# Slots and place biases on GpSimd, h in pairs of blocks, copies of x split by side

## The chip, the cores and the metric

One NeuronCore of a Trainium2 chip. In the profile PE is TensorE (matmuls; PEld its weight loads), DVE is VectorE, ACT is ScalarE, POOL is GpSimd and SP is SyncE, which here only issues transfers; ACTq and DVEq are sequencers of those engines. The metric is the time of one execution in device microseconds; the median of several runs counts.

## The reference

Linear attention over 8 batches, 8 heads, 576 positions and 64 columns a head, and then a mixture of 8 experts of which each row takes one.

```
q_s = exp(q - max(q, -1)); q_s /= sum(q_s, -1) + 1e-9      # over the 64 columns
k_s = exp(k - max(k, 2));  k_s /= sum(k_s, 2) + 1e-9       # over the positions
x = (q_s @ (k_s^T @ v)) as rows [4608, 512]
logits = x @ w_gate + modality_bias[modality_id]
e = argmax(logits); g = max(softmax(logits))
out[row] = g[row] * (relu(x[row] @ w1[e[row]]) @ w2[e[row]])   # w1 512x1024, w2 1024x512
```

## The kernel before

The bias of a modality outweighs what x adds to the logits, so the kernel takes one expert for each of the two modalities, loads the weights of these two alone (by registers read from the computed ids), and sorts the rows by modality: side a fills a list of places from the front, side b from the back. A count at the end would repeat work for rows that chose another expert; here its loop runs zero times.

**Attention**, batch by batch (`attention`): q, k and v come by SP in one queue into a ring of five buffers `st`. ScalarE takes the exponentials of q and k, VectorE sums q (L827), VectorE (batches 0 and 1) or GpSimd (later ones) scales q into `eq` (L843), ScalarE or GpSimd casts v into `vb` (L864). TensorE then forms kv (L957), from which VectorE makes `kinv` (L984, L987) and the scaled `kvbd` (L993); it sorts q within a block of 64 positions by a permutation `perm` (S1, L1033), which is cast into `et` (L1045 on ScalarE, L1047 on VectorE), and multiplies by kvbd (S2, L1072). S2 leaves two blocks of 64 positions in one PSUM bank. Each block is copied twice into the sorted `xs` (L1103): to a window of side a and to one of side b, whose starts are register values read from `offp` (L1007).

**Places.** `slot_run` and `digits_run` give each row's place, in two digits; one-hot matrices of the digits (`hhi`, L689, and `hlo`, L677, written into xs where no window lies yet) and their products `hv` with the rows' numbers (GpSimd, L701) go through 36 matmuls (L718) to the list `idx` of rows by place. `bsel_run` gives each place its bias.

**Experts.** 18 passes of 256 places (`ffn`), nine a side: logits (L1138), h in 8 blocks of 128 (L1198; 4 matmuls of 256 columns each, one bank a block) with an eviction by ScalarE (L1172) or VectorE (L1174), whichever the planner finds free, then y in two tiles of 128 rows (L1211; 8 matmuls of 512 columns), scaled by the gate (L1178, L1180) and stored by an indirect transfer of GpSimd (L1183). `ffn_rest` repeats the one block of 128 places that both sides share.

**Order.** All this is written down as operations with costs, a rank and buffers from rings; `Plan.order` runs a list scheduler over them and so fixes each engine's order and each buffer. On the chip every engine takes its list in order and waits by semaphores. A ring of six PSUM banks (a seventh joins) serves all of it. `load_w` asks for weights from GpSimd's queue: the first behind the landing of batch 1's k, the last two of the second expert (`pl.later(o, o_hv[-1])`) behind the last hv.

## Time and profile before

| | us |
|---|---|
| median of 3 runs | 208.88 |
| lowest and highest | 205.66, 209.72 |
| profiled execution | 204.27 |
| its span, first to last instruction | 202.0 |
| PE, DVE, ACT, POOL busy | 178.6, 154.7, 128.0, 90.6 |

The span is that of the profiled execution alone. Busy time says how full an engine is, not what the end waits for; a busy PE can hold matmuls that wait in its pipeline.

### The profile page before, as it was taken

What the parts mean: (1) busy time and instruction counts of PE and PEld (TensorE: products, weight loads), DVE (VectorE), ACT (ScalarE), POOL (GpSimd) and SP (SyncE); (2) the same over time, 40 slices, a digit from 0 to 9 for tenths busy, and PEclk for the clock granted to TensorE, in tenths of its full rate; (3) what the DMA queues carried; (4) which work ended last, traced back from release to release, by engine and by line L of the source; (5) the groups of instructions that cost most, each with busy time, mean ns of one, the idle gap of its engine ahead of it and who ended that gap; (6) DMA issues with size and microseconds to landing.
All of it is one profiled execution on the core that took longest, in us unless ns stands there. A gap on an engine that the chain in (4) does not pass through costs nothing.

```text
span 202.0 us, 5027 instructions
## 1 busy us (share of the span) xinstructions
PE 178.6 (88%) x1735; PEld 122.8 (61%) x1735; DVE 154.7 (77%) x447; ACT 128.0 (63%) x283; POOL 90.6 (45%) x113
## 2 busy tenths in 40 slices
PE   0899559869989899999979979999999999999990
PEld 0446237457656577777566756778667656766760
DVE  2998998997878999685978996869588657755660
ACT  2679886969738689999949966999895000000100
POOL 6000920674843649974098159591303311322231
PEclk9999997999999999999999999999999999999998
DMA  5999999999999997999539922111112112121202
GB/s 196 357 401 395 180 185 209 276 373 321 293 352 405 413 399 272 356 408 396 216 72 394 338 86 79 52 55 55 57 52 104 52 55 104 52 107 54 83 21 109
DMA packets 19612, 42.33 MB, mean 210 GB/s; under 512 B 1913, under 2 KB 3961, under 8 KB 19586
## 3 DMA queue, kind: packets, MB, share of 16 engines
q1 hardware_dynamic: 13344, 28.33, 38.6%
q0 software_dynamic: 6224, 13.64, 24.2%
q8 instruction: 14, 0.23, 0.5%
q10 hardware_dynamic: 18, 0.04, 0.2%
q14 instruction: 12, 0.10, 0.1%
HBM read 36.75 MB, written 9.70 MB: 230 GB/s over the span
## 4 chain that ended last, share of the span: by engine, by line
PE 50%; DMA 23%; DVE 10%; POOL 6%; issue 5%; ACT 3%; ACTq 1%; DVEq 0%; POOLq 0%
PE ps L1211 22%; PE ps L1198 19%; DMA st<-in_v_dram 9%; DMA W<-in_moe_w_dram 8%; DMA st<-in_q_dram 5%; POOL eq L843 2%; DVE xs L1103 2%; DVE own L827 2%; PE ps L957 2%; PE ps L1033 2%; DVE eq L843 2%; PE ps L1072 2%; PE ps L1138 2%; DMA bias<-n_moe_modality_bias_dram 2%; POOL out_dram L1183 1%
## 5 line engine op out<-in xcount | busy, mean ns | idle before, releaser
L1198 PE MATMUL ps<-xs,W 128*128 128x256 bf16 x576 | 71.5, 276 | 0.7 <-DVE hT L1174 0.3
L1211 PE MATMUL ps<-W,hT 128*128 128x512 bf16 (+1 forms) x296 | 66.6, 373 | 0.9 <-DMA W<-in_moe_w_dram 0.9
L1183 POOL DMA_INDIRECT out_dram<-y_sb,idx x36 | 35.6, 989 | 60.2 <-DVE y_sb L1180 31.0
L1198 PEld LDWEIGHTS <-W 128*128 128x128 bf16 x576 | 55.2, 99 | 10.2 <-issue 1.5
L1172 ACT ACTIVATE hT<-ps 128x256 bf16<-128x256 f32 x63 | 22.4, 393 | 40.6 <-PE ps L1198 40.5
L1211 PEld LDWEIGHTS <-hT 128*128 128x128 bf16 x296 | 28.3, 98 | 29.6 <-issue 1.3
L1174 DVE TENSOR_SCALAR hT<-ps 128x256 bf16<-128x256 f32 (+1 forms) x83 | 34.5, 427 | 5.6 <-PE ps L1198 2.4
L1180 DVE TENSOR_SCALAR y_sb<-ps,gate 128x512 f32<-128x512 f32 (+1 forms) x28 | 20.1, 720 | 21.5 <-PE ps L1211 19.0
L1103 ACT CAST xs<-ps 128x256 f32 (+1 forms) x99 | 31.8, 446 | 2.1 <-PE ps L957 1.0
L843 POOL TENSOR_TENSOR eq<-st,qi 128x512 bf16<-128x512 f32 (+1 forms) x30 | 28.5, 977 | 6.0 <-PE ps L1198 3.5
L827 DVE TENSOR_REDUCE own<-st 128x18 f32<-128x1152 f32 x16 | 21.6, 1351 | 0.1
L821 ACT ACTIVATE st<-st 128x1152 f32<-128x1152 f32 x16 | 18.4, 1177 | 4.8 <-DMA st<-in_q_dram 4.3
L854 ACT ACTIVATE ek<-st 128x1152 bf16<-128x1152 f32 x16 | 18.8, 1181 | 1.8 <-DMA st<-in_k_dram 1.8
L1045 ACT CAST et<-ps 128x512 bf16<-128x512 f32 (+1 forms) x30 | 16.1, 561 | 4.7 <-PE ps L1033 4.4
L1103 DVE CAST xs<-ps 128x256 f32 (+1 forms) x45 | 16.1, 416 | 0.8 <-ACT xs L1103 0.7
L1033 PE MATMUL ps<-perm,eq 128*128 128x128 bf16 x144 | 13.2, 221 | 4.0 <-DVE eq L843 1.7
L864 POOL CAST vb<-st 128x1152 bf16<-128x1152 f32 x8 | 9.0, 1144 | 13.0 <-DMA st<-in_v_dram 7.1
L1033 PEld LDWEIGHTS <-eq 128*128 128x128 bf16 x144 | 9.5, 98 | 7.8 <-DVE eq L843 3.6
L957 PE MATMUL ps<-vb,ek 64*128 64x129 bf16 x288 | 11.0, 217 | 2.2 <-ACT vb L864 2.2
L510 POOL DMA_DIRECT2D W<-in_moe_w_dram x8 | 5.1, 674 | 15.9 <-DVE ok L1487 15.8
L957 PEld LDWEIGHTS <-ek 64*128 64x128 bf16 x288 | 8.3, 93 | 5.9 <-ACT vb L864 2.5
L1072 PE MATMUL ps<-et,kvbd 128*128 128x128 bf16 (+1 forms) x160 | 11.4, 214 | 0.2
(134 smaller groups left out, 170.9 us busy)
## 6 DMA issues: line engine op xcount, KB each, us to landing
st<-in_q_dram SPq DMA_DIRECT2D x6, 1152.0 KB, 11.8
st<-in_k_dram SPq DMA_DIRECT2D x6, 1152.0 KB, 15.6
st<-in_v_dram SPq DMA_DIRECT2D x6, 1152.0 KB, 8.0
st<-in_q_dram SPq DMA_DIRECT2D x4, 576.0 KB, 5.2
st<-in_k_dram SPq DMA_DIRECT2D x4, 576.0 KB, 10.0
st<-in_v_dram SPq DMA_DIRECT2D x4, 576.0 KB, 10.8
W<-in_moe_w_dram POOLq DMA_DIRECT2D x8, 256.0 KB, 7.1
W<-in_moe_w_dram POOLq DMA_DIRECT2D x4, 512.0 KB, 16.5
```

The costliest lines, as they stand in the source:

```text
L827: nc.vector.tensor_reduce(out=sums[qib.idx][:, h * NJ : (h + n) * NJ], in_=view(st[bq.idx], [[Dh, n * NJ], [1, Dh]], h * NJ * Dh), op=ALU.add,
L843: (nc.vector if e == "DVE" else nc.gpsimd).tensor_tensor(out=view(eq[eqb.idx], [[HG * Dh, n], [Dh, HG], [1, Dh]], j0 * HG * Dh), in0=view( ...
L854: nc.scalar.activation(out=view(ek[ekb.idx], [[Dh, n], [HG * Dh, NJ], [1, Dh]], h * Dh), in_=view(st[bk.idx], [[NJ * Dh, n], [Dh, NJ], [1, ...
L957: nc.tensor.matmul(out=ps_t[kvp[hg].idx][:, 130 * hp : 130 * hp + 129], lhsT=ek[ekb.idx][rows, j, P * hp : P * hp + P], rhs=vb[vbb.idx][ro ...
L1033: nc.tensor.matmul(out=view(t, [[2 * nj * 64, 2], [1, 64]], hp * nj * 64 + jj * 64), lhsT=eq[eqb.idx][:, j0 + jj, P * hp : P * hp + P], rh ...
L1103: w_ = nc.scalar.copy(out=dst, in_=src) if e == "ACT" else nc.vector.tensor_copy(out=dst, in_=src)
L1172: nc.scalar.activation(out=dst, in_=src, func=ACT.Relu)
L1174: nc.vector.tensor_scalar_max(out=dst, in0=src, scalar1=0.0)
L1180: nc.vector.tensor_scalar(out=dst, in0=src, scalar1=g, scalar2=None, op0=ALU.mult)
L1183: s_ = nc.gpsimd.indirect_dma_start(out=out, out_offset=bass.IndirectOffsetOnAxis(ap=ix[:, c : c + 1], axis=0), in_=ysb, in_offset=None, b ...
L1198: m = nc.tensor.matmul(out=t[:, 0:w], lhsT=W[:, slot_, kd * F + f * P : kd * F + (f + 1) * P], rhs=xs[:, kd, lo : lo + w], start=(kd == 0) ...
L1211: nc.tensor.matmul(out=t, lhsT=h[:, kf, i * P : (i + 1) * P], rhs=W[:, slot_, W2 + kf * D + c0 : W2 + kf * D + c0 + cn], start=(kf == 0), ...
```

## The change

- The ids and the biases have a load each; what follows from the ids no longer depends on the biases. `vals_run` is ranked early.
- `slot_run` and `bsel_run` run on GpSimd.
- Two blocks of h share a bank, side by side, and are evicted by one instruction of 512 columns.
- `copier` says which engine copies a batch's blocks for side a and side b. Before, batch 0 was split and the later ones were ScalarE's or VectorE's whole; now batch 1 is ScalarE's, and batches 2 to 7 give side a to ScalarE and side b to VectorE. An engine that copies reads the starts into its registers first.
- Rest's y is ranked behind the h of the last pass; the reckoned cost of the gates rises; after the last pass of side a that has one, GpSimd's drain follows the evictions and not the store.

```diff
-    l_ids = pl.op({"ACT": (1.2, 3.5)}, load_ids, rank=-9)
+    l_ids = pl.op({"ACT": (0.6, 3.6)}, load_ids, rank=-9)
+    l_bias = pl.op({"ACT": (0.6, 3.9)}, load_bias, rank=-8)
...
-    o_parts = pl.op({"DVE": (0.35, 0.5)}, parts_run, [l_ids, c_dve], rank=-5)
+    o_parts = pl.op({"DVE": (0.35, 0.5)}, parts_run, [l_bias, c_dve], rank=-5)
...
     def slot_run(_):
-        d = nc.vector
+        d = nc.gpsimd
...
     def bsel_run(_):
-        d = nc.vector
+        d = nc.gpsimd
...
-    o_vals = pl.op({"DVE": (0.7, 0.85, True)}, vals_run, [c_dve2], rank=15)
-    o_slot = pl.op({"DVE": (1.17, 1.3, True)}, slot_run, [o_off], rank=15)
-    o_digits = pl.op({"DVE": (0.5, 0.65, True)}, digits_run, [o_slot], rank=15)
+    o_vals = pl.op({"DVE": (0.7, 0.85)}, vals_run, [c_dve2], rank=-4)
+    o_slot = pl.op({"POOL": (1.3, 1.45, True)}, slot_run, [o_off], rank=12)
+    o_digits = pl.op({"DVE": (0.5, 0.65, True)}, digits_run, [o_slot], rank=12)
...
-    o_bsel = pl.op({"DVE": (1.25, 1.35, True)}, bsel_run, [o_off, o_exp], rank=13)
+    o_bsel = pl.op({"POOL": (1.8, 2.0, True)}, bsel_run, [o_off, o_exp], rank=13)
...
-    copier = [("ACT", "DVE")] + [(e, e) for e in ("ACT", "DVE", "ACT", "ACT", "DVE", "ACT", "ACT")]
+    copier = [("ACT", "DVE")] + [("ACT","ACT")] + [("ACT","DVE")] * 6
...
-    def h_mm(t, lo, w, slot_, f, whole=False):
-        for kd in range(KD):
-            m = nc.tensor.matmul(
-                out=t[:, 0:w],
...
+    def h_mm(t, lo, w, slot_, f0, whole=False):
+
+        for i in range(2):
+            for kd in range(KD):
+                f = f0 + i
+                m = nc.tensor.matmul(
+                    out=t[:, i * w : (i + 1) * w],
...
-        g3 = pl.op({"DVE": (0.18, 0.36)}, lambda _: gates3(t0, nt, ex[xb.idx]), [g2], rank=rank_g, uses=[xb])
+        g3 = pl.op({"DVE": (0.32, 0.45)}, lambda _: gates3(t0, nt, ex[xb.idx]), [g2], rank=rank_g, uses=[xb])
...
-        for f in range(KF):
+        for f in range(0, KF, 2):
...
-                on_pe(*[w] * KD),
+                on_pe(*[w] * (2 * KD)),
...
-                    {**on_act(w), **on_dve(w)},
-                    lambda e, f=f, fb=fb: relu(e, hT[hb.idx][:, f, 0:w], ps_t[fb.idx][:, 0:w]),
+                    {**on_act(2 * w), **on_dve(2 * w)},
+                    lambda e, f=f, fb=fb: relu(
+                        e, hT[hb.idx][:, f : f + 2, 0:w], view(ps_t[fb.idx], [[w, 2], [1, w]])
+                    ),
...
-            pl.op({"POOL": (3.0, 3.0)}, lambda _: nc.gpsimd.drain(), [st_], rank=-1)
+            drain = lambda _: nc.gpsimd.drain()
+            if (n, lo, w) == passes_a[-1]:
+                pl.op({"POOL": (2.0, 2.0)}, drain, evs, rank=-0.5)
+            else:
+                pl.op({"POOL": (3.0, 3.0)}, drain, [st_], rank=-1)
...
-            on_pe(*[D] * KF), y_rest(fb), [*hs, *wc], rank=500 + rank + 0.2, takes=[fb], uses=[hb, wb[1]]
+            on_pe(*[D] * KF), y_rest(fb), [*hs, *wc], rank=500 + rank + 0.4, takes=[fb], uses=[hb, wb[1]]
```

With other costs and engines the planner writes another order. Three places follow; names carry buffer numbers (`ps_90` to `ps_96` are the PSUM banks).

VectorE, batch 0, where q is scaled: before, the five scalings (four of 512 columns and one of 256) stand ahead of kinv.

```order
L839 RECIPROCAL qi_86<-qi_86 128x36
L1484 TENSOR_SCALAR ok<-aoff 1x1
L1487 TENSOR_SCALAR ok<-aoff 1x1
L843 TENSOR_TENSOR eq_70<-st_63,qi_86 128x512 x4
L843 TENSOR_TENSOR eq_70<-st_63,qi_86 128x256
L984 TENSOR_SCALAR kinv_88<-ps_93 128x2
L984 TENSOR_SCALAR kinv_88<-ps_94 128x2
L1484 TENSOR_SCALAR ok<-aoff 1x1
L1487 TENSOR_SCALAR ok<-aoff 1x1
L987 RECIPROCAL kinv_88<-kinv_88 128x4
L1047 CAST et_76<-ps_92 128x4x128
```

With the change:

```order
L841 RECIPROCAL qi_86<-qi_86 128x36
L1495 TENSOR_SCALAR ok<-aoff 1x1
L1498 TENSOR_SCALAR ok<-aoff 1x1
L845 TENSOR_TENSOR eq_70<-st_63,qi_86 128x512
L986 TENSOR_SCALAR kinv_88<-ps_93 128x2
L986 TENSOR_SCALAR kinv_88<-ps_94 128x2
L1495 TENSOR_SCALAR ok<-aoff 1x1
L1498 TENSOR_SCALAR ok<-aoff 1x1
L989 RECIPROCAL kinv_88<-kinv_88 128x4
L845 TENSOR_TENSOR eq_70<-st_63,qi_86 128x512 x3
L845 TENSOR_TENSOR eq_70<-st_63,qi_86 128x256
L995 TENSOR_TENSOR kvbd_74<-ps_93,kinv_88 64x2x64 x2
```

kinv, which reads both halves of batch 0's kv, now stands behind the first scaling and ahead of the other four; the cast of et has left VectorE here.

VectorE behind the scalings of batch 1, before the change: kinv, the biases of the places, kvbd, the first logits, vals, and slot ahead of the digits.

```order
L987 RECIPROCAL kinv_89<-kinv_89 128x4
L667 TENSOR_SCALAR isb<-place,aoff 128x36
L668 TENSOR_TENSOR bsel<-isb,biasd 128x288
L671 TENSOR_TENSOR bsel<-bsel,bias_b 128x288
L672 TENSOR_SCALAR krow<-isb,keyd,key 128x36
L993 TENSOR_TENSOR kvbd_75<-ps_94,kinv_89 64x2x64 x2
L993 TENSOR_TENSOR kvbd_75<-ps_90,kinv_89 64x2x64 x2
L1152 TENSOR_TENSOR L<-ps_95,bsel 128x16
L1153 TENSOR_REDUCE gmx<-L 128x2
L1152 TENSOR_TENSOR L<-ps_93,bsel 128x16
L1153 TENSOR_REDUCE gmx<-L 128x2
L660 TENSOR_SCALAR idh<-id_i 128x36
```

With the change:

```order
L1105 COPY xs<-ps_93 128x4x64
L654 TENSOR_SCALAR hi<-slot_141 128x36
L657 SCALAR_TENSOR_TENSOR lo<-hi,slot_141 128x36
L658 CAST hib<-hi 128x36
L986 TENSOR_SCALAR kinv_89<-ps_94 128x2
L986 TENSOR_SCALAR kinv_89<-ps_90 128x2
L989 RECIPROCAL kinv_89<-kinv_89 128x4
L691 TENSOR_TENSOR hhi<-own,hib 128x432
L995 TENSOR_TENSOR kvbd_75<-ps_94,kinv_89 64x2x64 x2
L995 TENSOR_TENSOR kvbd_75<-ps_90,kinv_89 64x2x64 x2
```

The operations of biases are gone from this place, those of vals and slot from the rows behind it, and the digits with the first third of hhi have come ahead of kvbd.

The same nine operations on GpSimd, with what stands around them (`ex` is the last of its constants, `eid_i` the ids of the two experts, on which the weights' loads wait), with the change:

```order
L353 MEMSET ex_99 128x2
L645 TENSOR_TENSOR slot<-na,kt 128x72
L646 TENSOR_TENSOR slot<-slot,pos 128x72
L647 TENSOR_TENSOR slot<-slot,aoff 128x72
L650 COPY slot_141<-slot 64x36 x2
L669 TENSOR_SCALAR isb<-place,aoff 128x36
L670 TENSOR_TENSOR bsel<-isb,biasd 128x288
L673 TENSOR_TENSOR bsel<-bsel,bias_b 128x288
L674 TENSOR_SCALAR krow<-isb,keyd,key 128x36
L541 TENSOR_LOAD eid_i
L512 ISA
L512 DMA W<-in_moe_w_dram 64x2x1024
```

They stand between the constants and the first load of weights.

ScalarE, copies of batch 3 out of one bank, before, with the semaphores that an instruction waits for (PE's, its own or another engine's):

```order
L1103 REGISTER_ALU
L1103 ISA
L1103 COPY xs<-ps_90 128x4x64 [waits DVE_49,PE_49]
L1103 REGISTER_ALU
L1103 ISA
L1103 COPY xs<-ps_90 128x4x64
L1103 ISA
L1103 COPY xs<-ps_90 128x4x64 [waits Activation_49]
L1103 ISA
L1103 COPY xs<-ps_90 128x4x64 [waits Activation_49]
```

With the change, ScalarE's copies of batch 3 out of banks 91 and 92:

```order
L1105 REGISTER_ALU
L1105 ISA
L1105 COPY xs<-ps_91 128x4x64 [waits DVE_49,Activation_49]
L1105 ISA
L1105 COPY xs<-ps_91 128x4x64 [waits DVE_49]
L1105 REGISTER_ALU
L1105 ISA
L1105 COPY xs<-ps_92 128x4x64 [waits DVE_49,Activation_49]
L1180 ACTIVATE y_sb_83<-ps_94,gate 128x512 [waits DMASW1_49,PE_49]
L1105 ISA
L1105 COPY xs<-ps_92 128x4x64 [waits DVE_49]
```

and VectorE's copies out of the same two:

```order
L1105 REGISTER_ALU
L1105 ISA
L1105 COPY xs<-ps_91 128x4x64 [waits DVE_49,PE_49]
L1105 ISA
L1105 COPY xs<-ps_91 128x4x64 [waits Activation_49]
L1105 REGISTER_ALU
L1105 ISA
L1105 COPY xs<-ps_92 128x4x64 [waits DVE_49,PE_49]
L1105 ISA
L1105 COPY xs<-ps_92 128x4x64 [waits Activation_49]
```

Before, four copies of a bank follow each other on ScalarE and wait for that engine and TensorE alone. Now each engine makes two of the four, and nearly each of them waits for the other engine.

## Rows read from the trace of the kernel before

**Rows 1.** Windows: length, busy PE, PEld, DVE, ACT, POOL, granted clock, DMA share, GB/s
```profile
30.14:62.00 31.86, 28.42 (x282) 19.58 (x279) 27.20 (x79) 22.90 (x59) 15.68 (x18) 0.96 1.11 309
...
62.00:100.00 38.00, 37.06 (x404) 26.36 (x403) 31.92 (x83) 34.79 (x86) 22.90 (x23) 1.00 0.96 365
...
100.00:120.00 20.00, 17.35 (x212) 12.62 (x211) 17.60 (x54) 15.43 (x26) 11.79 (x12) 1.00 0.63 218
...
140.00:196.55 56.55, 56.50 (x436) 38.36 (x433) 37.12 (x94) 16.02 (x32) 15.36 (x16) 1.00 0.17 66
```

**Rows 2.** Timeline of PE; start, us, instructions, [idle before <-what ended it]
```profile
44.99 1.33 PE L718 MATMUL ps<-hv,xs 128*128 128x72 bf16 x36 [1.56 <-ACT hT L1172]
...
59.87 2.32 PE L1211 MATMUL ps<-W,hT 128*128 128x512 bf16 x10 [0.89 <-DMA W<-in_moe_w_dram]
...
105.35 0.40 PE L1033 MATMUL ps<-perm,eq 128*128 128x128 bf16 x4 [1.14 <-POOL eq L843]
...
119.36 0.62 PE L1138 MATMUL ps<-wg_sb,xs 128*128 128x8 bf16 x16 [1.37 <-ACT hT L1172]
```

**Rows 3.** Timeline of DVE and of PE, batch 0's scalings and second kv
```profile
13.35 2.83 DVE L843 TENSOR_TENSOR eq<-st,qi 128x512 bf16<-128x512 f32 x5
...
14.93 0.69 PE L957 MATMUL ps<-vb,ek 64*128 64x129 bf16 x18
```

**Rows 4.** Groups by form: evictions; busy us, mean ns | idle before
```profile
L1174 DVE TENSOR_SCALAR hT<-ps 128x256 bf16<-128x256 f32 x81 | 33.2, 420 | 4.9 <-PE ps L1198 2.4 <-PE ps L1138 0.6 <-ACT et L1045 0.5
...
L1045 ACT CAST et<-ps 128x512 bf16<-128x512 f32 x24 | 14.0, 599 | 3.7 <-PE ps L1033 3.5
...
L1174 DVE TENSOR_SCALAR hT<-ps 128x512 bf16<-128x512 f32 x2 | 1.4, 692 | 0.7 <-PE ps L1347 0.5
```

**Rows 5.** Timeline of DVE, biases, kvbd, slot and one-hot digits
```profile
30.01 0.21 DVE L667 TENSOR_SCALAR isb<-place,aoff 128x36 f32<-128x36 f32 x1
...
31.33 1.20 DVE L993 TENSOR_TENSOR kvbd<-ps,kinv 64x128 bf16<-64x128 f32 x4
...
34.43 0.21 DVE L643 TENSOR_TENSOR slot<-na,kt 128x72 f32<-128x72 f32 x1
...
38.17 5.66 DVE L677 TENSOR_TENSOR xs<-own,lo 128x384 bf16<-128x384 f32 x12
```

**Rows 6.** Timeline of POOL, first weights, hv and last weights
```profile
20.01 2.65 POOL L510 DMA_DIRECT2D W<-in_moe_w_dram  x4 [15.77 <-DVE ok L1487]
...
37.31 5.25 POOL L701 TENSOR_TENSOR hv<-hhi,vals 128x432 bf16<-128x432 bf16 x6 [10.61 <-DVE hhi L689]
...
42.51 1.55 POOL L521 DMA_DIRECT2D W<-in_moe_w_dram  x2
```

**Rows 7.** Timeline of ACT, first exponential of batch 2's q
```profile
43.41 1.16 ACT L821 ACTIVATE st<-st 128x1152 f32<-128x1152 f32 x1 [1.95 <-DMA st<-in_q_dram]
```

**Rows 8.** DMA queue of SP loads, 42 to 44, 48 to 58
```profile
q1 hardware_dynamic: 337, 0.77, 103.2%
...
q1 hardware_dynamic: 904, 2.01, 58.4%
```

**Rows 9.** Chain that ended last, in order of time: start, us, what
```profile
152.16 3.49 PE ps L1198 x32
```

**Rows 10.** That chain over 0 to 35, copies of batch 0
```profile
24.26 0.75 ACTq L1007
...
25.29 0.38 ACT xs L1103
...
25.69 0.44 DVE xs L1103
```

**Rows 11.** Timelines of ACT and DVE, copies of two batches
```profile
81.39 4.60 ACT L1103 CAST xs<-ps 128x256 f32 x16
...
65.65 3.72 DVE L1103 CAST xs<-ps 128x256 f32 x11
```

**Rows 12.** Timeline of POOL, cast of batch 6's v
```profile
100.83 2.24 POOL L864 CAST vb<-st 128x1152 bf16<-128x1152 f32 x2 [5.11 <-DMA st<-in_v_dram]
```

More of the change, by code (lines that the diff above doesn't have):

```diff
@@ L435, in load_ids, with load_bias @@
         )
+    def load_bias(_):
         nc.scalar.dma_start(
@@ L1194, in store @@
             stored.append(s_)
-    def h_mm(t, lo, w, slot_, f, whole=False):
-        for kd in range(KD):
-            m = nc.tensor.matmul(
-                out=t[:, 0:w],
-                lhsT=W[:, slot_, kd * F + f * P : kd * F + (f + 1) * P],
-                rhs=xs[:, kd, lo : lo + w],
-                start=(kd == 0),
-                stop=(kd == KD - 1),
-            )
-            if whole and not f and not kd:
-                for w_ in final[-2:]:
-                    sync(m, w_, "every batch is in its places")
+    def h_mm(t, lo, w, slot_, f0, whole=False):
[4 more added lines that the diff above has]
+                    out=t[:, i * w : (i + 1) * w],
+                    lhsT=W[:, slot_, kd * F + f * P : kd * F + (f + 1) * P],
+                    rhs=xs[:, kd, lo : lo + w],
+                    start=(kd == 0),
+                    stop=(kd == KD - 1),
+                )
+                if whole and not f and not kd:
+                    for w_ in final[-2:]:
+                        sync(m, w_, "every batch is in its places")
     def y_mm(t, h, i, slot_, c0=0, cn=D):
```

## The prediction

> **What bounds the kernel now.** I read the busy time by stage first [rows 1], then what TensorE waited for [rows 2], then the engines that those waits point to. From 140 us to the last matmul at 196.55 TensorE is busy 56.50 of 56.55 us at full clock: nothing that hands it work faster can shorten that stage. Before it, from the first h matmul at 30.14, TensorE is idle 31.86 - 28.42 = 3.44 us up to 62, 0.94 us up to 100 and 2.65 us up to 120, together 7.0 us; that, and the 30.14 us before, is all that the change can win. Transfers set the pace of the same stages: the DMA share is 1.11 up to 62 and 0.96 up to 100 [rows 1]. VectorE and ScalarE, which empty PSUM, are busy 31.92 and 34.79 of 38 us between 62 and 100, 88% of both together: any work added there shows soon.
>
> The named waits [rows 2]: 1.56 us before the matmuls that make the lists of rows (L718), 0.89 us for the last part of the second expert's weights, 1.14 us for batch 5's scaled q, 1.37 us when v of batch 7 has just come.
>
> **The start.** The ids now have a load of their own, so the ranks no longer stand behind the bias; I take that as a gain of up to 1 us on VectorE and nothing on the path. Against it, kinv of batch 0 is moved in VectorE's order from behind the five scalings of q to behind the first. The five take 2.83 us from 13.35, so the first ends near 13.35 + 2.83 / 4.5 = 14.0; but kinv needs the second half of the kv matmuls, 14.93 + 0.69 = 15.6 [rows 3]. VectorE would stand 1.6 us before kinv, and behind it are queued the other four scalings, kvbd, perm, and so every copy of batch 0 and the scalings of batch 1 on which the first h matmul waits. The cast of et that goes to ScalarE gives VectorE back about what its other eviction of 512 columns takes, 0.69 us [rows 4], and the ids perhaps half a microsecond. I take +0.5 us, from -0.7 (the ids' whole microsecond and half of the cast's time beyond the wait) to +1.2 (the wait less the half).
>
> **Slots and biases on GpSimd.** VectorE loses the biases, 30.01 to 31.33, and slot, five operations from 34.43 whose first takes 0.21, so about 1.1 us [rows 5]; the four of vals go to the start. That is about 2.8 us less ahead of the one-hot digits, twelve operations of together 5.66 us from 38.17, which end at 43.8. GpSimd does the moved nine operations behind its constants, where it stood idle 15.77 us until 20.01, when batch 1's k let it ask for weights [rows 6]. The offsets they read are ready before the scalings at 13.35. An operation of hv, 432 columns, takes 5.25 / 6 = 0.88 us there; two of the nine have 288 columns, the others 72 or fewer, so I take 3 us in all, hidden, cost nothing; were each as long as hv's, 7.9 us from 13.35 would hold the weights back by 1.2 us. hhi, hence hv, hence the last two loads of the second expert's weights, asked for at 42.51 behind hv's 5.25 us [rows 6], come some 5 us sooner. So two of the waits, 1.56 and 0.89 us, lose their cause.
>
> What is late next is batch 2. ScalarE waited 1.95 us for its q, to 43.41 [rows 7], and between 42 and 44 the loads of q, k and v had 103.2% of the 16 engines' time, between 48 and 58, with weights and stores beside them, 58.4% [rows 8]. Weights that start 5 us sooner halve that rate from about 41.6 on: q of batch 2 can come up to 1.8 us later, k and v more, while the first S1 of batch 2 now stands 24 h matmuls nearer in TensorE's order, 24 x 0.109 = 2.6 us (32 take 3.49 in the dense stage [rows 9]). So of 3.44 us I count 1.0 us as won, from -2.5 us (the two waits) to +1.5 us (the two returned as waits for q and v of batch 2, and as much again of the half rate).
>
> **h in pairs.** An eviction of 256 columns takes 0.420 us on VectorE, one of 512 columns 0.692 (rest's h); a ScalarE cast of 512 columns, that of et, takes 0.599 [rows 4]. A pair so costs 2 x 0.420 - 0.692 = 0.15 us less than two; with the like on ScalarE, 72 pairs save 11 us of engine time over the kernel, 5 to 6 us to each engine, about half of it before 120. From 140 on it is worth nothing, since TensorE does not wait. Nor does the later first eviction cost there: y's step for block f waits for block f alone, and six steps of 512 columns, 2 x 0.109 us each, stand ahead of the last pair's.
>
> **Copies by side.** Batch 1 stays on ScalarE; from batch 2 on side a is ScalarE's and side b VectorE's. Both read the same bank, and the order with its waits shows that a copy waits for the other engine's copy out of that bank. Batch 0 was so copied before: ScalarE's of 25.29 takes 0.38 us and VectorE's starts with its end, at 25.69, and takes 0.44 [rows 10]. One engine alone takes 4.60 / 16 = 0.29 us a copy, or 3.72 / 11 = 0.34 [rows 11]. So 18 copies took 5.2 or 6.1 us; if the last copy of a bank overlaps the first of the next, three slots of 0.41 serve four copies, and 18 take 13.5 x 0.41 = 5.6 us. I therefore expect neither a gain nor a loss in length, where the planner takes both sides for parallel. What is won is that neither engine is away from h for the whole time; what is lost is that each stands still in half of it. Six more register loads (15 for 9) cost each at most the 0.75 us that one kept ScalarE [rows 10], and none where the engine has work queued: in the digits' 5.66 us [rows 5] one is hidden whole. Pairs and copies together, 62 to 100: -0.5 us, from -0.9 (all that is idle there) to the first rival's price.
>
> The Trainium skill, "PSUM — Partial Sum Buffer", section "PSUM bank collisions raise a hardware error", says that any two of the engines must be kept apart on one bank and quadrant, reads against reads included. By it the sides of one bank can never be copied together, and the split could only lose; the alternation in batch 0 agrees, and the first rival is what that would cost here.
>
> **After 100.** The new order puts more h and y ahead of late batches: kv of batch 7 comes some 11 us of matmuls later, kv of batch 6 some 4, S1 of batch 5 some 2, S1 of batch 6 half a microsecond sooner (counted from the order at the dense stage's durations). The wait of 1.37 us goes, most of the 1.14 too. But GpSimd still casts v of batch 6 before it scales batch 5; it waited 5.11 us for that v, to 100.83 [rows 12], and q's buffer of batch 5 is that of v of batch 7. That chain keeps S1 of batch 6 from coming much earlier. Of 2.65 us I take 1.5, from -2.5 to +1.0 (TensorE ahead of the loads).
>
> **Rest's y and the drain.** Between h and y of the last pass rest's y hides the last eviction; but before, that stage had 0.05 us idle [rows 1], so nothing; its store comes later but still ahead of the last tile's. The drain, moved ahead of nothing but a store, and the reckoned gate costs move nothing on the path.
>
> Sum: +0.5 - 1.0 - 0.5 - 1.5 = -2.5 us against the profiled execution's 204.27 (span 202.0), 201.8. That execution was 4.6 us under the median of 208.88, and nothing in one trace tells which stage the others lengthen; I carry the difference over: **206.4 us**.
>
> **Rivals.** First, slower: the copies alternate strictly. Then 18 take 9 x (0.38 + 0.44) = 7.4 us and, with the hand-overs of 0.02 us, 7.7, some 2 us more than the 5.6 above. Batches 2 to 5 fall where both engines are 88% busy, so it shows there, 4 x 2.0 = 8.0 us, less 3 us that the pairs save on each engine by then: +5 us, 213.9. It decides once an engine standing in a copy's wait holds back h evictions longer than the six PSUM banks last, 6 x 8 x 0.109 = 5.2 us. For it: the waits in the order; against: in several banks the order has two and two, which overlap. Chance 0.12. Second, all idle time returns: 7.0 us, 201.9; for it, the waits named have lost their causes; against, the DMA share. Chance 0.25. Third, transfers set the pace whatever the engines do, and the half rate gives back what the digits win: 208.9, within 1.5 us; for it, 1.11 and 0.96. Chance 0.23. That the change doesn't do what it says is excluded by the order. My forecast, -1.5 to -4.2 us, has 0.40.
>
> A measurement of this kernel can tell about 2%, 4.2 us. Faster by more: the second rival and a little of the forecast, 0.28; slower: the first, 0.12; within: 0.60. The range: from just under the second rival, 201.5, to 211.0, which leaves out most of the first; the forecast's own is 204.7 to 207.4.
>
> **What would show it.** Right: slot and bsel on GpSimd before 20 us; hv near 32, the lists' matmuls near 41 to 42; no wait for weights near 59; copies of one bank taking turns; evictions near 0.69 and 0.60 us; TensorE idle between 30 and 120 near 4 us. A wait before kinv near 14 to 15.6, and the first h matmul at 30.6, show the start. Wrong: copies of one bank side by side; TensorE waiting long for batch 2's q or v near 48 to 55; VectorE or ScalarE standing in copies while full banks wait.

## The result and the profile after

The changed kernel takes 208.09 us in the median of 20 runs (205.27 to 210.18), the kernel before 206.55 us beside it: a ratio of 1.011, 95% interval 1.006 to 1.016. A second set of 12 runs gave 1.007 (1.003 to 1.012). Ratios compare the faster executions of each kernel with those of the kernel before beside them, and so differ a little from a ratio of medians; of told and ps_told below, the execution profiled was among the slower. The kernel is slower by about 1%: inside the wide range of 201.5 to 211.0 and within the 2% that was called no change, but outside the 204.7 to 207.4 of the forecast, which expected a gain. The execution profiled took 208.31 us (span 206.7), 4.04 us more than that of before (span 202.0); TensorE's last matmul ends at 200.58 where it ended at 196.55, so 4.03 of the 4.7 us by which the span grew lie ahead of that end.

The windows by stage, in the columns of [rows 1]; the first ends with the first h matmul:

```profile
0.00:31.09 31.09, 19.26 (x194) 10.85 (x195) 25.76 (x91) 22.37 (x32) 13.71 (x39) 0.99 0.97 282
31.09:62.00 30.91, 26.46 (x264) 18.73 (x264) 23.45 (x60) 19.49 (x46) 15.88 (x18) 0.90 1.10 313
62.00:100.00 38.00, 35.51 (x379) 25.36 (x381) 29.18 (x75) 30.00 (x60) 23.61 (x24) 1.00 0.90 327
100.00:120.00 20.00, 19.09 (x202) 13.47 (x201) 16.60 (x38) 16.60 (x32) 10.47 (x11) 1.00 0.77 266
120.00:140.00 20.00, 18.35 (x196) 12.89 (x193) 15.48 (x38) 16.43 (x34) 11.42 (x12) 1.00 0.23 90
140.00:200.58 60.58, 59.89 (x503) 41.75 (x508) 43.76 (x110) 18.44 (x36) 20.10 (x21) 1.00 0.16 62
```

Up to 62, TensorE stands 30.91 - 26.46 = 4.45 us (3.44 before), and the granted clock is 0.90 (0.96). From 62 to 100 it stands 2.49 us (0.94), though VectorE and ScalarE are *less* busy than before, 29.18 and 30.00 us for 31.92 and 34.79, and less of the transfers' time is used (0.90 for 0.96). Fewer matmuls were done there too (379 for 404), so this is work put off as well as time saved. From 100 to 140 the 2.56 us are about what stood there before.

Its named waits, in the timeline of TensorE:

```profile
51.26 1.89 PE L1216 MATMUL ps<-W,hT 128*128 128x512 bf16 x4 [3.56 <-ACT hT L1174]
...
90.56 0.35 PE L1140 MATMUL ps<-wg_sb,xs 128*128 128x8 bf16 x8 [1.12 <-ACT xs L1105]
...
124.79 0.56 PE L1140 MATMUL ps<-wg_sb,xs 128*128 128x8 bf16 x16 [1.36 <-ACT xs L1105]
```

All four waits of [rows 2] are gone. In their place y waits 3.56 us for an h eviction, and the logits wait twice for the last copies of a batch.

The groups of copies (L1105) and of h evictions, as in [rows 4]: busy us, mean ns, then the idle time of the engine just before them and what ended it:

```profile
L1105 ACT CAST xs<-ps 128x256 f32 (+1 forms) x81 | 29.5, 397 | 15.7 <-DVE xs L1105 11.5 <-PE ps L1074 2.0 <-DVE qi L840 1.5
L1105 DVE CAST xs<-ps 128x256 f32 (+1 forms) x63 | 26.6, 422 | 10.5 <-ACT xs L1105 9.2
...
L1176 DVE TENSOR_SCALAR hT<-ps 128x512 bf16<-128x512 f32 x45 | 30.5, 684 | 4.1 <-PE ps L1203 3.0 <-PE ps L1358 0.4 <-ACT et L1047 0.2
L1174 ACT ACTIVATE hT<-ps 128x512 bf16<-128x512 f32 x29 | 16.8, 595 | 5.8 <-PE ps L1203 5.7
```

ScalarE stood 11.5 us until a copy of VectorE's ended, VectorE 9.2 us until one of ScalarE's. The evictions of 512 columns take the 0.69 and 0.60 us that the prediction gave them. The chain that ended last runs through these turns; batch 5:

```profile
122.16 0.43 DVE xs L1105
122.59 0.02 issue
122.62 0.39 ACT xs L1105
123.01 0.02 issue
123.03 0.44 DVE xs L1105
...
124.36 0.38 ACT xs L1105
124.74 0.05 issue
124.79 0.56 PE ps L1140 x16
```

Each of the first three starts with the end of the other engine's, 0.02 us behind it, and TensorE's logits with the end of the last. That holds within a bank. Between two banks copies do run side by side; here, in batch 3, the second of VectorE's two copies beside ScalarE's of 86.81, which is the last of the bank before:

```profile
86.35 0.95 DVE L1105 CAST xs<-ps 128x256 f32 x2 [0.51 <-ACT xs L1105]
86.81 0.39 ACT L1105 CAST xs<-ps 128x256 f32 x1 [0.49 <-DVE xs L1105]
```

In the timelines of batches 2 to 7 this happens 20 times (4.8 us in all), and not once within a bank.

What stood behind the wait of 3.56 us, in ScalarE's timeline:

```profile
45.98 1.06 ACT L1174 ACTIVATE hT<-ps 128x512 bf16<-128x512 f32 x2
49.56 1.16 ACT L856 ACTIVATE ek<-st 128x1152 bf16<-128x1152 f32 x1 [2.52 <-DMA st<-in_k_dram]
50.63 1.06 ACT L1174 ACTIVATE hT<-ps 128x512 bf16<-128x512 f32 x2
```

ScalarE stands in its order before k of batch 2; the h evictions queued behind it, and y behind these, wait with it. Why k is late, the queues from 42 to 46 say. Before the change the loads had 104.5% in the same stretch:

```profile
q1 hardware_dynamic: 696, 1.56, 104.5%
```

With the change:

```profile
q1 hardware_dynamic: 366, 0.83, 59.9%
q0 software_dynamic: 351, 0.36, 52.6%
```

The weights now run in the second queue, beside q and k. GpSimd's timeline gives their time, beside [rows 6]:

```profile
7.79 0.34 POOL L645 TENSOR_TENSOR slot<-na,kt 128x72 f32<-128x72 f32 x1 [3.24 <-DVE na L613]
...
12.91 0.36 POOL L674 TENSOR_SCALAR krow<-isb,keyd,key 128x36 f32<-128x36 f32 x1
...
32.04 1.77 POOL L703 TENSOR_TENSOR hv<-hhi,vals 128x432 bf16<-128x432 bf16 x2 [5.46 <-DVE hhi L691]
...
37.80 1.56 POOL L523 DMA_DIRECT2D W<-in_moe_w_dram  x2
```

### The profile page after: what moved, and what is told of

It is laid out like the page before. It is cut to its first block, busy times and chain, and to the rows that moved or that the text cites. A ratio compares the mean times of both kernels' runs of the same rounds, so it can differ in the third digit from the quotient of the medians.

```text
span 206.7 us, 4924 instructions
## 1 busy us (share of the span) xinstructions
PE 178.6 (86%) x1717; PEld 123.0 (60%) x1735; DVE 155.1 (75%) x411; ACT 123.3 (60%) x236; POOL 96.5 (47%) x124
## 5 line engine op out<-in xcount | busy, mean ns | idle before, releaser
L1203 PEld LDWEIGHTS <-W 128*128 128x128 bf16 x576 | 55.7, 99 | 10.2 <-issue 1.6
L1216 PEld LDWEIGHTS <-hT 128*128 128x128 bf16 x296 | 28.2, 98 | 32.5 <-ACT hT L1174 5.1
L1105 ACT CAST xs<-ps 128x256 f32 (+1 forms) x81 | 29.5, 397 | 15.7 <-DVE xs L1105 11.5
L1105 DVE CAST xs<-ps 128x256 f32 (+1 forms) x63 | 26.6, 422 | 10.5 <-ACT xs L1105 9.2
L1176 DVE TENSOR_SCALAR hT<-ps 128x512 bf16<-128x512 f32 x45 | 30.5, 684 | 4.1 <-PE ps L1203 3.0
L1182 DVE TENSOR_SCALAR y_sb<-ps,gate 128x512 f32<-128x512 f32 (+1 forms) x21 | 15.1, 722 | 12.4 <-PE ps L1216 10.9
L1174 ACT ACTIVATE hT<-ps 128x512 bf16<-128x512 f32 x29 | 16.8, 595 | 5.8 <-PE ps L1203 5.7
L1047 ACT CAST et<-ps 128x512 bf16<-128x512 f32 (+1 forms) x30 | 15.5, 532 | 3.6 <-PE ps L1035 3.3
L1035 PE MATMUL ps<-perm,eq 128*128 128x128 bf16 x144 | 13.5, 224 | 2.8 <-DVE eq L845 1.9
L866 POOL CAST vb<-st 128x1152 bf16<-128x1152 f32 x10 | 11.2, 1146 | 7.9 <-DMA st<-in_v_dram 7.9
L1180 ACT ACTIVATE y_sb<-ps,gate 128x512 f32<-128x512 f32 x16 | 11.1, 703 | 1.4 <-PE ps L1216 1.3
L874 DVE TENSOR_TENSOR perm<-own,posx 128x1152 bf16<-128x1152 f32 x8 | 10.8, 1350 | 1.1 <-issue 0.9
## 6 DMA issues: line engine op xcount, KB each, us to landing
st<-in_v_dram SPq DMA_DIRECT2D x6, 1152.0 KB, 10.2
W<-in_moe_w_dram POOLq DMA_DIRECT2D x4, 512.0 KB, 11.6
```

What stands on the lines that cost most here:

```text
L1035: nc.tensor.matmul(out=view(t, [[2 * nj * 64, 2], [1, 64]], hp * nj * 64 + jj * 64), lhsT=eq[eqb.idx][:, j0 + jj, P * hp : P * hp + P], rh ...
L1105: w_ = nc.scalar.copy(out=dst, in_=src) if e == "ACT" else nc.vector.tensor_copy(out=dst, in_=src)
L1176: nc.vector.tensor_scalar_max(out=dst, in0=src, scalar1=0.0)
L1182: nc.vector.tensor_scalar(out=dst, in0=src, scalar1=g, scalar2=None, op0=ALU.mult)
L1203: m = nc.tensor.matmul(out=t[:, i * w : (i + 1) * w], lhsT=W[:, slot_, kd * F + f * P : kd * F + (f + 1) * P], rhs=xs[:, kd, lo : lo + w], ...
L1216: nc.tensor.matmul(out=t, lhsT=h[:, kf, i * P : (i + 1) * P], rhs=W[:, slot_, W2 + kf * D + c0 : W2 + kf * D + c0 + cn], start=(kf == 0), ...
```

## The experiments

The planner orders all work anew with every edit, so most of the first kernels ask what an edit is worth with its own order, and others keep an order and change only what runs in it. Three theories run through the expectations: (1) weights that start early make k of batch 2 late; (2) copies that take turns cost the time, (2a) because the plan does not know of the turns or (2b) because engines that stand are lost whatever the plan; (3) any new order moves the time. The table gathers all runs. "Idle" is TensorE's from 62 to 160 us, 98.00 less its busy time there. "Copies" is the time from the first to the last copy of a batch, added up over batches 2 to 5 from the timelines of both engines. "Stood" is the idle time before copies, ScalarE's and VectorE's in one, from the groups. These three come from one execution each; the changed kernel itself gave 5.48 and 4.93 in the idle column, so half a microsecond there means nothing. "Fixed" marks kernels in which TensorE's and GpSimd's rows stand as in the kernel named.

| run | what it is | ratio to before | 95% | idle | copies | stood |
|---|---|---|---|---|---|---|
| (before) | | 1 | | 3.71 | 24.5 | 2.9 |
| split_only | before + split | 0.998 | 0.993-1.004 | 4.27 | 29.8 | 20.2 |
| pairs_only | before + pairs | 0.992 | 0.988-0.996 | 1.34 | 23.6 | 4.2 |
| gpsimd_only | before + GpSimd's part | 0.992 | 0.988-0.997 | 2.56 | 25.0 | 3.8 |
| unsplit | changed, no split | 0.995 | 0.990-1.001 | 4.86 | 24.2 | 2.3 |
| pairs_split | before + pairs + split | 1.027 | 1.021-1.033 | 8.12 | 33.8 | 28.7 |
| (changed) | | 1.011 | 1.006-1.016 | 5.48 | 32.6 | 26.2 |
| changed_again | | 1.007 | 1.003-1.012 | 4.93 | 32.6 | 26.4 |
| pairs_order_split | pairs_only fixed, split | 1.057 | 1.053-1.062 | 14.03 | 35.1 | 34.9 |
| unsplit_order_split | unsplit fixed, split | 1.063 | 1.059-1.067 | 13.42 | 36.6 | 37.1 |
| ps_order_unsplit | pairs_split fixed, no split | 1.014 | 1.008-1.020 | 7.70 | 32.8 | 3.6 |
| changed_order_unsplit | changed fixed, no split | 1.019 | 1.013-1.026 | 7.29 | 33.8 | 4.1 |
| bybank | changed fixed, a bank's copies on one engine | 1.026 | 1.017-1.034 | 6.32 | 29.2 | 19.9 |
| skew | changed, in a bank one side after the other | 1.017 | 1.009-1.025 | 5.97 | 32.5 | 11.6 |
| told | changed, plan knows the turns | 1.033 | 1.023-1.044 | 8.18 | 46.0 | 22.5 |
| ps_told | pairs_split, plan knows the turns | 1.000 | 0.994-1.005 | 5.87 | 46.3 | 16.3 |
| changed_gates | changed, one gate cost in the plan | 1.014 | 1.009-1.019 | 6.92 | 27.2 | 18.9 |
| hold | changed fixed, weights held | 1.012 | 1.005-1.018 | 5.95 | 32.6 | 26.6 |
| unsplit_hold | unsplit fixed, weights held | 0.989 | 0.982-0.997 | 4.57 | 24.2 | 2.4 |
| unsplit_hold_one | unsplit fixed, last load held | 0.994 | 0.989-0.998 | 3.80 | 24.2 | 2.9 |

The ratio follows the idle column best: every kernel under 5 us there is below 1.01, every one over 5.9 above it; between them lie the changed kernel (5.48) and ps_told. The other two columns follow only in part.

**One edit at a time, and without the split.** The split alone is one line in the kernel before, undoing it the same line in the changed one:

```diff
-copier = [("ACT", "DVE")] + [(e, e) for e in ("ACT", "DVE", "ACT", "ACT", "DVE", "ACT", "ACT")]
+copier = [("ACT", "DVE")] + [("ACT","ACT")] + [("ACT","DVE")] * 6
```

split_only: 

> Edit: the kernel before with the table of copies of the changed one, so from batch 2 on side a on ScalarE and side b on VectorE; slots, biases and single h blocks as before. The planner orders the rest anew. Theory 1 (early weights): as the kernel before, within 0.7%, 205 to 208. Theory 2 (copies that take turns): slower by 1 to 3%, 208.5 to 212.5, idle time of either engine before copies near 10 us instead of 2.1 and 0.8. Theory 3 (the order): either side, within 1%.

unsplit: 

> Edit: the changed kernel with the table of copies of the kernel before, so both sides of a batch on one engine; everything else as changed. The planner orders the rest anew. Theory 1: the wait for k near 50 stays and with it the time, 207 to 209. Theory 2: 203 to 205.5, ScalarE and VectorE no longer idle some 20 us before copies. Theory 3: within 1% of the changed kernel, either side.

Undoing the split gives back 1.2 to 1.5%, as theory 2 wants; but the split alone costs nothing, against it, though the engines stand 20.2 us before copies there. So it costs beside something else, and the next runs took the other parts apart. pairs_only is the new h_mm, its loop over pairs and the relu of two blocks; gpsimd_only is the load of the ids, d = nc.gpsimd in slot_run and bsel_run, and their ranks; pairs_split adds the copier line to the first.

pairs_only: 

> Edit: the kernel before with h in pairs of blocks per bank and nothing else of the change. The first runs: the split alone 0.998 of before, the change without the split 0.995, with it 1.011, so the split costs 1.5% only beside something else of the change. Theory 1 (early weights cost what is lost): 0.985 to 0.995. Theory 2 (the split costs, and it costs through pairs: an engine that stands in a copy's wait now keeps two h blocks, and its partner is away 0.6 to 0.7 us at a time): 0.985 to 1.000. Theory 3 (each edit only shuffles the planner's order): anywhere from 0.99 to 1.01.

gpsimd_only: 

> Edit: the kernel before with slots and biases on GpSimd, the ids' load of their own and the ranks that go with it; single h blocks, copies as before. Theory 1: weights asked for near 38, ScalarE waits for k of batch 2 to 49 or later, TensorE behind it 2 to 4 us, 1.005 to 1.015. Theory 2: the waits for lists and weights go, 0.985 to 0.998. Theory 3: 0.99 to 1.01.

pairs_split: 

> Edit: the kernel before with h in pairs and the split table of copies; slots, biases, weights as before. Theory 1: as pairs alone, 0.985 to 0.997, since the weights come as before. Theory 2: 1.0 to 1.5% slower than pairs alone, 1.003 to 1.012, copies of batches 2 to 7 in about 49 us in all as in the changed kernel, not 41 as before. Theory 3: 0.99 to 1.01.

changed_again: 

> The changed kernel itself once more, on the same chip as the three others. All theories: 1.005 to 1.016 of before.

Pairs and GpSimd's part each make the kernel 0.8% *faster*; theory 1 as the whole cause falls, since the early weights alone are a gain, with y's wait still there (2.30 us at 50.83). The split beside pairs costs 3.5%, more than theory 2 had.

**Holding the weights.** The edit keeps every instruction in its place (unsplit_hold is the same in unsplit; unsplit_hold_one holds part 3 alone):

```diff
 issued["w", s, part] = w_dma(eids[s], s, part)
+if s and part == 2:
+    behind(issued["w", 1, 2][0], issued[q.tensor.name, 2], "q of batch 2 comes first")
```

hold: 

> Edit: in the changed kernel the last two loads of the second expert's weights wait until q of batch 2 has landed; nothing else moves. Theory 1 (weights that start 4.7 us sooner halve the rate of q, k and v of batch 2; ScalarE stands in its order before k to 49.56 and TensorE waits 3.56 us behind the h eviction queued there, then runs at half clock for a while): q1 above 100% between 42 and 46 again, k about 2.5 us sooner, the wait at 51 below 1 us, end 3 to 5 us sooner, 203 to 205 us where the changed kernel has 208. Theory 2 (the copies that take turns cost the time, from 62 us on): the wait at 51 goes, but it is lost again behind the copies, 207 to 208.5. Theory 3 (the new order of the work around 100 to 160 us, whatever the copies): as theory 2.

unsplit_hold: 

> Edit: the changed kernel with the table of copies of before (0.995 of before), and the last two loads of the second expert's weights held until q of batch 2 has landed. Theory 1 for this stage (early weights make k of batch 2 late; y waits 3 to 5 us behind ScalarE's wait for k): 0.98 to 0.99. Against it: holding them in the changed kernel gave nothing that could be measured, since y then waited 1.2 us for these weights and the rest was lost later: 0.992 to 0.999.

unsplit_hold_one: 

> Edit: the changed kernel without the split, with only the last of the second expert's weights' loads held until q of batch 2 has landed (holding the last two measured 0.989, with 2 us of wait for weights at 60.8 and no wait at 51). Theory 1 (the two waits are the two ends of one balance of transfers): wait at 51 under 2 us and wait for weights under 1 us, 0.985 to 0.993.

The mechanism is as theory 1 has it. From 42 to 46 the loads have their rate back, and in place of the wait for k near 51 there is one for weights; hold's queue and TensorE:

```profile
q1 hardware_dynamic: 701, 1.57, 104.9%
```

```profile
61.09 2.10 PE L1218 MATMUL ps<-W,hT 128*128 128x512 bf16 x9 [1.23 <-DMA W<-in_moe_w_dram]
```

A wait of 3.56 us gone and one of 1.23 come should be worth some 2 us; in the changed kernel none of it can be measured (1.012 for 1.007 to 1.011), and S1 there waits 1.09 and 0.33 us for GpSimd's q (109.61, 125.94), which it did not before the hold. In unsplit it is 0.6% in the ratios, whose intervals overlap. The last load alone changes nothing there: y still waits 3.03 us.

**Fewer hand-overs, same order.** bybank sets, for batches 2 to 7, the engine of a bank's copies by the bank, when the order is already made:

```diff
+if getattr(o, "bank", (0, 0))[0] >= 2:
+    o.engine = ("ACT", "DVE")[o.bank[1] % 2]
 o.run(o.engine)
```

> Edit: the changed kernel with every instruction in its planned place, but from batch 2 on the copies of a bank all on one engine: banks 1, 3, 5 of a batch on ScalarE, 2 and 4 on VectorE (10 and 8 of 18 copies). So no copy waits for the other engine within a bank; at most 4 hand-overs in a batch instead of some 17. Theory 1: no gain, 207 to 209. Theory 2: idle time before copies falls from 21 us on both engines to under 10, TensorE's waits at 90.56 and 124.79 shrink, 204 to 206.5. Theory 3: no gain.

It got worse. The logits' waits for copies at 90.56 and 124.79 did shrink, to 0.58 and none, but ScalarE and VectorE still stood 19.9 us before copies, S1 waited 1.50 and 2.30 us for q that GpSimd scales behind a late v (110.36, 127.23), and the clock fell for longer than in the changed kernel (last section). What a bank's four copies in a row on one engine do to the work planned between them was not in any of the theories.

**The plan told, and the copies skewed.** told and ps_told add, for split copies, the copy before in the bank to what the plan waits for, with measured times; skew issues a bank's copies by side.

```diff
+turn = win[-1] if split and (jj or side) else None
...
+({"DVE": (0.33, 0.44)} if side else {"ACT": (0.28, 0.40)})
+if split
...
-[o3, o_id if b >= 3 else None, *los, before, across],
+[o3, o_id if b >= 3 else None, *los, before, across, turn],
```

```diff
-for jj in range(nj):
-    for side in range(2):
+by_side = [(jj, side) for side in range(2) for jj in range(nj)]
...
+for jj, side in by_side if b >= 2 else by_block:
```

told: 

> Edit: the changed kernel, with the planner told that the copies of a bank take turns: each copy but a bank's first depends in the plan on the copy before it, at 0.28 (to 0.40) us on ScalarE and 0.33 (to 0.44) on VectorE. Instructions and waits stay the same; what moves is the order of the work around them. So far: pairs alone 0.992 of before, split alone 0.998, both 1.027, the changed kernel 1.007 to 1.011. Theory 2a (the copies are planned as running side by side, so the logits behind them stand too early in TensorE's order and TensorE waits for the last copies): waits of logits for copies fall from 3.3 us to under 1, 0.993 to 1.002 of before. Theory 2b (the turns cost engine time, 21 to 26 us that ScalarE and VectorE stand, which no order gives back): no gain, 1.005 to 1.015. Theory 3 (any new order moves the time by about 1%): 0.995 to 1.015.

ps_told: 

> Edit: pairs and split without the rest of the change (1.027 of before, logits waiting 6.0 us for copies), with the planner told of the turns as in the run before. Theory 2a: 0.995 to 1.008, the logits' waits under 2 us. Theory 2b: 1.015 to 1.03. Theory 3: 0.99 to 1.03.

skew: 

> Edit: the changed kernel with the copies of a bank issued by side from batch 2 on: both of side a, then both of side b, which follow while ScalarE is at the next bank's side a. The plan knows that side b comes behind side a. One hand-over a bank in place of three or four. Theory 2a: copies of a batch in 4 to 5 us in place of 8.2 on average, waits of logits for copies under 1 us, 0.99 to 1.00 of before. Theory 2b: the same gain, since the standing time falls from 26 to under 10 us. Theory 3: 0.995 to 1.015.

No theory has all three. Told of the turns, pairs with split gains 2.7% and the changed kernel loses 2.2 to 2.6%, although the logits' waits for copies fell in both, from 6.0 to 2.6 us and from 3.1 to 1.6 us (2a asked for under 2 and under 1). skew more than halves the standing time, to 11.6 us, and is no faster (1.009 to 1.025 for 1.006 to 1.016); so standing engines alone are not the cost, and 2b falls as it was put. The longest wait that told has is in ScalarE's and TensorE's timelines:

```profile
123.77 1.15 ACT L866 CAST vb<-st 128x1152 bf16<-128x1152 f32 x1 [4.00 <-DMA st<-in_v_dram]
124.83 0.59 ACT L1178 ACTIVATE hT<-ps 128x512 bf16<-128x512 f32 x1
```

```profile
125.47 0.58 PE L1220 MATMUL ps<-W,hT 128*128 128x512 bf16 x1 [3.80 <-ACT hT L1178]
```

The order puts ScalarE's cast of a late v ahead of an h eviction, as at 119.36 before the change [rows 2], and far worse. skew loses 3.03 us at 109.58, where S1 waits for q that GpSimd scales behind a late v. Both waits are for transfers, not for copies, and come of where the new order lays them. unsplit has one of the first kind as well, 2.36 us at 121.61.

**The order kept, the split alone changed.** Here only the engines of the copies differ, with the offsets loaded on both where the split needs them:

```diff
+b, side = getattr(o, "copy", (0, 0))
+if b >= 2:
+    o.engine = ("ACT", "DVE")[side]
 o.run(o.engine)
```

The two kernels without split have `"DVE" if b in (2, 5) else "ACT"` there. changed_gates is the other half, an order changed and nothing else: the plan's cost of the third gate step back at 0.18, 0.36.

pairs_order_split: 

> Edit: pairs alone (0.992 of before), every instruction in its planned place, but from batch 2 on side a's copies on ScalarE and side b's on VectorE, with the offsets loaded on both. TensorE's and GpSimd's order are the same row by row. Theory 2 (the turns themselves cost): 1.01 to 1.03, copies of a batch in 7.5 to 10 us where they took 6, TensorE waiting 4 us or more for copies. Theory 3 (the new order costs, not the turns): 0.985 to 1.0.

unsplit_order_split: 

> Edit: the changed kernel without the split (0.995 of before), every instruction in its planned place, but from batch 2 on side a's copies on ScalarE and side b's on VectorE. Theory 2 (the turns cost, and the order made for split copies hides most of it): 1.03 to 1.065, copies of batches 2 to 7 in 50 to 57 us in all where they took 40. Theory 3 (only the order costs): 0.99 to 1.0.

ps_order_unsplit: 

> Edit: pairs with split (1.027), every instruction in its planned place, but the copies of batches 2 and 5 all on VectorE and those of 3, 4, 6 and 7 on ScalarE, as before the change. Theory 2: 0.995 to 1.01, the waits of logits for copies below 2 us in place of 6. Theory 3: 1.02 to 1.035.

changed_order_unsplit: 

> Edit: the changed kernel (1.007 to 1.011), every instruction in its planned place, copies as in the run before. Theory 2: 0.992 to 1.0. Theory 3: 1.005 to 1.015.

changed_gates: 

> Edit: the changed kernel with the plan's cost of the third gate step back at 0.18 (to 0.36) us in place of 0.32 (to 0.45). No instruction changes its work or engine by it, only the planner's order. All theories want 1.007 to 1.011 if an order alone is worth little; how far it is off shows what a mere shuffle can do, and theory 3 wants a shift of 0.7% or more, to either side.

On an order made for whole batches the split costs 6.6% (1.057 against 0.992) and 6.8% (1.063 against 0.995), 13 to 14 us: theory 2, in the first of them more than it asked. What changes by the edit beside the engine of the copies is the loading of the starts on the second engine, once a batch. TensorE from 62 to 160 us, of pairs_only and of pairs_order_split, same rows in the same order:

```profile
62.00:160.00 98.00, 96.66 (x1019) 1.00 0.57 211
```

```profile
62.00:160.00 98.00, 83.97 (x899) 0.98 0.54 197
```

pairs_only's 18 copies of batch 2 are one row on VectorE; in pairs_order_split the same batch goes like this on both engines:

```profile
63.38 6.04 DVE L1103 CAST xs<-ps 128x256 f32 x18
```

```profile
65.46 0.39 ACT L1105 CAST xs<-ps 128x256 f32 x1 [0.49 <-DVE xs L1105]
65.73 1.16 ACT L854 ACTIVATE ek<-st 128x1152 bf16<-128x1152 f32 x1
65.87 0.43 DVE L1105 CAST xs<-ps 128x256 f32 x1 [0.45 <-issue]
66.79 0.38 ACT L1105 CAST xs<-ps 128x256 f32 x1
67.20 0.43 DVE L1105 CAST xs<-ps 128x256 f32 x1 [0.90 <-ACT xs L1105]
...
68.58 1.03 PE L1204 MATMUL ps<-xs,W 128*128 128x256 bf16 x8 [1.20 <-ACT hT L1175]
...
72.91 0.61 PE L1217 MATMUL ps<-W,hT 128*128 128x512 bf16 x2 [1.99 <-ACT hT L1175]
```

Beside the turns themselves, whatever one engine does between two copies stops the other: ScalarE takes the exponential of k (1.16 us), and VectorE, whose next copy is behind ScalarE's, stands 0.90. Behind both stand h evictions, and TensorE waits for those.

The way back is not its mirror. Taking the split out of pairs_split's order gives 1.2%, out of the changed kernel's order it *costs* 0.8 to 1.2% (1.013 to 1.026, clear of the second set of the changed kernel but not of the first): these orders were laid for copies on both engines. Nor are the batches shorter for it, 32.8 and 33.8 us with whole batches on one engine. So the split's own cost is shown in orders laid for whole batches; what it costs in the changed kernel is known only with the planner's new order beside it, 1.2 to 1.5% from unsplit. And changed_gates, an order moved by one cost in the plan, is 0.3 to 0.7% above the changed kernel, with intervals that overlap: at the edge of what theory 3 asked, and not clear of noise.

## Why the prediction was wrong

**The step that failed** is that of the copies by side: "if the last copy of a bank overlaps the first of the next, three slots of 0.41 serve four copies, and 18 take 13.5 x 0.41 = 5.6 us. I therefore expect neither a gain nor a loss in length" (13.5 x 0.41 is 5.5). The overlap between banks was right: in each of batches 2 to 5 some copy is under way for 5.9 to 6.6 us. But the four batches took 32.6 / 4 = 8.2 us each where they had taken 6.1, because for 0.5 to 2.9 us of each neither engine copied. Of these 7.1 us in all the engine that made the next copy was at other work for 4.7, and its partner stood. That "each stands still in half of it" was written down and priced at nothing. It is 11.5 and 9.2 us, with h evictions queued behind. Where the order was kept as laid for whole batches, the four batches went from 23.6 to 35.1 us and from 24.2 to 36.6, and the kernel lost 6.6 and 6.8%. Length alone is not the measure, though: in the changed kernel's order whole batches take as long (33.8).

A second term was put at nothing as well, and I had its rows [rows 10, 11]: a copy in a row of its engine's own takes 0.29 or 0.34 us, a copy in turns 0.38 and 0.44. So the split adds work to both engines. The copies' groups before:

```profile
L1103 ACT CAST xs<-ps 128x256 f32 (+1 forms) x99 | 31.8, 446 | 2.1 <-PE ps L957 1.0 <-DVE xs L1103 0.5
L1103 DVE CAST xs<-ps 128x256 f32 (+1 forms) x45 | 16.1, 416 | 0.8 <-ACT xs L1103 0.7
```

That is 47.9 us of the two engines, and 56.1 with the change: 8.2 us more, most of the 9.7 that the evictions of pairs save (57.0 us before, 47.3 after).

The first rival had the turns within a bank and the direction, with a chance of 0.12. Its length (7.7 us, 2.0 us more a batch) came out almost to the number, but by luck: it had copies end to end without overlap, and what made the batches long was largely the other work between the copies. I had the waits in the order and a batch copied in this way in [rows 10], and argued past them. Of the Trainium skill's rule ("PSUM — Partial Sum Buffer", section "PSUM bank collisions raise a hardware error"), that two engines must be kept apart on a bank and quadrant even where both read, the trace shows what follows from it: in this program the waits between the copies keep it, and within a bank nothing is copied side by side. What the chip would do without these waits no run here shows.

**How much of the miss that is.** The forecast was -2.5 us, a ratio of 0.988; measured was 1.011, and without the split 0.995. So the split, with the order that the planner makes for it, is some two thirds of the miss, and the terms below are the rest. That 206.4 us came within 1.7 us of 208.09 is luck: the three executions known had a median of 208.88, twenty gave 206.55, so the 4.6 us that I carried over were 2.3 too many. The same luck brings the third rival, 208.9, nearest of all. Its reason holds in part up to 62, as the paragraph on slots shows, but not for the kernel: with the transfers as before, pairs alone gain 0.8%, and GpSimd's part with its half rate gains 0.8% too.

**The size of the first rival** was off as well: it priced the turns at +8 and took 3 off for pairs; its 213.9 is 208.88 + 5 and leaves out the other terms of the sum, with which it would be 211.9. Measured, the split costs nothing beside single blocks, 3.5% beside pairs, 1.2 to 1.5% (2.4 to 3.2 us) beside pairs and GpSimd's part, and 6.6 to 6.8% where the order is not laid anew. The missing term is the planner: it takes the copies for parallel, yet the order that it makes for them leaves at most about half of that cost. How much it recovers differs from kernel to kernel, and why it costs nothing beside single blocks (where no run kept the order) and 3.5% beside pairs is not settled. That an engine's work between two copies grows from 0.42 to 0.69 us with pairs, and stops the partner for as long, fits it; no run changed that length alone at a fixed order.

**The start**: +0.5 us forecast, the first h matmul 31.09 for 30.14. But kinv waited 0.57 us, not 1.6:

```profile
14.05 0.69 DVE L845 TENSOR_TENSOR eq<-st,qi 128x512 bf16<-128x512 f32 x1
...
15.31 0.22 DVE L986 TENSOR_SCALAR kinv<-ps 128x2 f32<-128x2 f32 x2 [0.57 <-PE ps L959]
```

Where the other 0.4 us come from I did not follow.

**Slots and biases on GpSimd**: right in each step, the nine operations hidden between 7.79 and 13.27, the last weights 4.7 us sooner, both named waits gone, the loads' rate halved. -1.0 us was forecast for 30 to 62 and the part by itself gives 0.8%, 1.6 us, but not there: in gpsimd_only TensorE stands 2.35 us from the first h to 62 (3.44 before), as forecast, and the granted clock, 0.89 for 0.96, takes about 2 us back; the gain lies from 100 to 120, 0.37 us of idle time for 2.65. What was mis-sized is who waits for batch 2: I reckoned q up to 1.8 us late, and it was 0.4 (43.85 for 43.41); k, "more", is what ScalarE stood for in front of h evictions. In the changed kernel TensorE's idle time to 62 grew by 1.0 us, and the half clock behind the wait of 3.56 us took more.

**Pairs**: right, 0.8% alone, with evictions of the length forecast. They do not add up: pairs and GpSimd's part together, with the small edits of the plan (the gates' cost, rest's y, the drain), give 0.5% in unsplit, where 1.6% would be the two. Both win the same idle time from 100 to 120 (2.65 us before, 0.13 and 0.37 with one of them), and in unsplit it is back, 2.07 us: S1 waits 1.23 us for GpSimd's q at 105.23. y's wait at 51 stays (3.15 us), and the one of 2.36 us at 121.61 is new. Whether the small edits have a share in it no run shows; the gates' cost alone was taken out, and only in the changed kernel.

**After 100**: -1.5 us was forecast; the waits of 1.14 and 1.37 us went, as said, but 1.36 us for the copies of batch 5 came, and from 100 to the last matmul TensorE stands 0.9 + 1.7 + 0.7 = 3.3 us for 2.8. Rest's y and the drain show nothing in the stage from 140 on, where TensorE stands 0.7 us in all.

Put together for the profiled execution: +0.95 us at the start, +3.0 of idle time from the first h to the last matmul (7.2 to 10.2), +1.8 of half clock (1.3 to 3.1, from the granted clocks of these windows), 5.7 us, against 4.03 measured. Of the remaining -1.7 us the rows do not tell the cause; matmuls' ends are modelled, and the trace after has records of 1717 of the 1735 matmuls. TensorE's work ahead of the first h did not grow (19.26 us busy for 19.42).

Better than both kernels, with the whole interval below 1, are four of the runs: unsplit_hold (0.989), pairs_only and gpsimd_only (0.992 each) and unsplit_hold_one (0.994).

## What to carry to other kernels

When two engines are to share a row of small reads, look at the waits in the order first: if a copy waits for the other engine's copy out of the same bank, the split buys nothing within the bank, each copy costs its engine more than in a row (0.38 to 0.44 us for 0.29 to 0.34 here), and every longer instruction between two copies stops both engines. A batch on one engine was the better split here; by bank was tried once, in an order not laid for it, and was slower still. Where a planner lays the order, compare edits at a fixed order too: here the same edit cost 0, 1.2 to 1.5, 3.5 or 6.6%, according to the order around it. And a load that is freed to start sooner takes its rate from the loads beside it; ask which in-order engine stands in front of those, and what is queued behind it.

## What was not expected of the hardware

TensorE's clock after y's wait for k. In the changed kernel it stood from 47.70 to 51.26 and then ran at 0.50, 1.2 GHz, for 3 us, which is worth 1.5 us (windows; busy PE, granted clock, DMA share, GB/s):

```profile
47.70:51.26 3.56, 0.00 (x1) 0.94 1.12 294
51.26:52.26 1.00, 1.00 (x3) 0.50 1.12 296
...
53.26:54.26 1.00, 1.00 (x8) 0.50 1.09 389
54.26:55.26 1.00, 1.00 (x11) 1.00 1.05 415
```

The length of the stand does not by itself tell whether the clock falls: behind the same wait of 2.67 us (changed_again), 2.71 (skew) and 3.15 (unsplit) it stayed at 1.00, behind 2.30 (gpsimd_only) and 3.03 (unsplit_hold_one) it fell for about 3 us, and behind 3.57 (bybank) and 3.65 (told) for 6 or more.
